# First batch's decays from sums of logarithms, its order written anew, and staged weights loaded next: one Trainium2 core

## The chip, the cores and the metric

The kernel runs on one core of a Trainium2 chip. The metric is the device time of one execution in microseconds (us), the median of several runs.

## What is computed

A gated linear attention feeds a mixer. Batch 4, 8 heads, 768 positions, head width 48; everything is float32, and the weights arrive as float64.

```
f = sigmoid(f_logit)
for t in range(S):
    state = f[t][:, None] * state + outer(k[t], v[t])     # for each batch and head, 48 x 48
    y[t]  = q[t] @ state
x = y as (batch, position, 384)
u = x + (x^T @ U @ V)^T                                   # rank 32, over the positions
out = u + relu(u @ w_ch1) @ w_ch2                         # 384 -> 1536 -> 384
```

## The kernel before

**Units.** A unit is two heads of one batch; a batch has HP = 4 units, all four have NU = 16. The 768 positions are cut into NCH = 12 chunks of 64, two chunks to a block of 128 (NBL = 6). Within a chunk the recurrence is written with two decays for each channel: X, the product of the gates from a position's successor to the end of the chunk, and Y, its counterpart for the queries, so that a key times X and a query times Y can be multiplied as matrices. `prepare(n)` (L643) makes them in five pieces: `gates` (L677) turns f with six transposes on TensorE and applies two sigmoids on ScalarE; `keep` (L692) makes X by a scan on VectorE that runs backwards (L694), copies the chunk totals to `least` (L699), and takes a floor, a reciprocal and a product for the later scan and the state (L701, L702, L704); `keys` (L706) turns k and multiplies it by X (L672); `read` (L710, under the name read_back in the order) makes Y by a second scan (L712); `queries` (L714) turns q and multiplies it by Y.

**Attention.** `attend(n)` (L770) has six pieces: `kept` (L802) turns the scaled keys back with twelve small transposes, copies them to kb (L813) and spreads the chunk totals to `whole` (L815); `states` (L817) multiplies kb by v and copies the sums to `added` (L833); `scan` (L838) carries the state over the chunks on VectorE (L848); `scores` (L780) multiplies keys by queries and masks them into A (L795); `read` (L855) multiplies the queries by the states (L865) and copies two columns to `seen` (L872); `inner` (L874) adds A times v (L883) and copies the result to x (L889). PSUM tiles of two banks rotate through three buffers (ps_big), and so a product waits until the tile of three before has been read.

**Order.** For the first batch the order is written out by hand (L979 to L998), and from there to the start of the second batch TensorE, VectorE and ScalarE execute exactly in the order of the program (manual_schedule, L966 and L967). `front(n, ...)` and `rear(n, ...)` fetch pieces of `prepare` and `attend`. `busy(3)` puts three filler products on TensorE in each turn. After the loop come the last unit's pieces, the weights of the low rank step and the mixer's start (L1001 to L1018); then the dense layer runs, `ch1` (L258) first, with the second batch's units between its pieces (L1024).

**Loads.** All loads are issued by SyncE, in program order: `load(n, names)` (L530) brings f, k, q, v of a unit. In the first batch each of f, k, q is loaded for the unit two later as soon as its own has been turned (`follow`, L651), v after the turn (L989).

**Weights.** Each weight slice is loaded raw as float64 and turned into float32 by `weight_loader`'s `end` (L83): two operations on ScalarE (L90, L91), three on VectorE (L92 to L94), one on GpSimd (L95). The list has U, two pieces of V (`early` = 3), twelve slices of w1 and twelve of w2. The first FIRST = 6 slices of w1 land in a tile of the dense layer that is still free (zw). Five weights are issued after the second turn (L993), four more after the loop (L997); from then on the end of one weight issues the one nine later (`ahead_by`, L103).

Of the kernel before, what the change touches and what calls it, by code (L numbers as in the profile page):

```python
# [10 lines left out]
F32 = mybir.dt.float32  # L11
# [14 lines left out]

LEAST = 1e-18

SMALLEST = struct.unpack("f", struct.pack("I", 896 << 20))[0]
# [443 lines left out]
def factored_path(ctx, tc, q, k, v, f_logit, moe_U, moe_V, moe_w_ch1, moe_w_ch2, out, ok):  # L473
# [49 lines left out]
    for slot in nat:  # L523
        for nm, t in slot.items():

            nc.gpsimd.memset(t[:, :, :, D:PAD], 20.0 if nm == "f" else 0.0)
    src = {"f": f_logit, "q": q, "k": k, "v": v}
# [30 lines left out]

    load(0, "f", "k", "q")
    load(1, "f")  # L560
    load(0, "v")
    load(1, "k", "q", "v")

    ident = const.tile([P, P], F32, name="ident")
# [33 lines left out]
    for i in range(2):  # L598
        nc.gpsimd.memset(wholes[i][:, 0:1], 0.0)

    table = one.tile([P, 1], F32, name="table")
    nc.scalar.activation(table, ident[:, 0:1], AF.Sigmoid)

# [39 lines left out]
    def prepare(n):  # L643
# [7 lines left out]
        def follow(nm):  # L651

            if n + 2 < NU and n + 2 not in (HP, HP + 1):
                load(n + 2, nm)
# [14 lines left out]
        def operand(nm, of):  # L669
            t = T[nm] = kz[n % 2][:, C:] if nm == "k" else two.tile([P, S], F32, name="qT")  # L670
            if n < TURNED:
                nc.vector.tensor_tensor(halves(t), on_tensor(nm), halves(T[of]), ALU.mult)  # L672
            else:
                turned(t, r[nm])
                nc.vector.tensor_tensor(t, t, T[of], ALU.mult)

        def gates():  # L677
# [36 lines left out]
        def queries():  # L714
            operand("q", "Y")
            follow("q")

        return [gates, keep, keys, read, queries]

# [247 lines left out]
    with tc.manual_schedule(engines={nc.vector.engine, nc.scalar.engine}):  # L967
# [4 lines left out]
        def busy(n):  # L972
            for _ in range(n):
                nc.tensor.matmul(idle[:, 0:DM], lhsT=ident, rhs=ends[:, 0:DM], start=True, stop=True)

        busy(1)
        for piece in front(0, "gates"):
            piece()
        for n in range(HP):  # L979
            pieces = front(n, "keep", "keys") + rear(n - 1, "scan", "scores")  # L980
            if n + 1 < HP:
                pieces += [lambda: busy(3)]
            pieces += rear(n, "kept") + front(n, "read_back", "queries")
            if n + 1 < HP:
                pieces += front(n + 1, "gates") + rear(n - 1, "read", "inner") + rear(n, "states")
            for piece in pieces:
                piece()
            if n < 2:
                load(n + 2, "v")  # L989
            if n == 1:  # L990


                for start, _ in weights[: early + 2]:  # L993
                    start()
            elif n > 1:
                load(n + 2, "f", "k", "q", "v")
        for start, _ in weights[early + 2 : early + FIRST]:  # L997
            start()  # L998


        loads = ahead_by(early + FIRST, weights)  # L1001
        done, rest = slice(0, 2 * n * D), slice(2 * n * D, DM)
        pieces = rear(n - 1, "read") + rear(n, "states") + rear(n - 1, "inner") + rear(n, "scan") + loads[:1]
        pieces += rear(n, "scores") + loads[1:2] + rear(n, "read") + loads[2 : early + 1]
        for piece in pieces:
# [3 lines left out]
        low_rank_of(done)  # L1009
        loads[early + 1]()  # L1010
        for piece in rear(HP - 1, "inner"):
# [3 lines left out]
        mix_of(done)  # L1015
        added_up_of(rest)
        mix_of(rest)
        loads = loads[early + 2 :]  # L1018

# [64 lines left out]
    lowest = one.tile([1, 1], F32, name="lowest")  # L1084
    nc.vector.tensor_reduce(lowest, lp[0:1, 0:P], AX.X, ALU.min)
    nc.vector.tensor_single_scalar(ok, lowest, LEAST, ALU.is_ge)
# [332 lines left out]
```

## Time and profile before

| | us |
|---|---|
| median of 3 runs | 485.11 |
| lowest, highest | 484.94, 485.13 |
| the profiled execution | 486.26 |
| its span, first to last instruction | 484.5 |
| PE busy in the span | 463.1 (96%) |
| VectorE busy | 358.2 (74%) |
| ScalarE busy | 170.7 (35%) |
| GpSimd busy | 37.7 (8%) |
| first dense matmul (L258) starts | 54.06 |

PE is TensorE's matmuls, PEld its weight loads, DVE is VectorE, ACT ScalarE, POOL GpSimd, SP SyncE. A busy PE is not PE at its peak, since matmuls are pipelined. A row of the groups names line, engine, operation, tiles and shapes; then busy time, mean ns of one, and the idle time before them with what ended it. A row of the timeline has start and length, and in brackets the idle time before it with its releaser.

### The profile page before, as it was taken

Reading aid. Unit: us, or ns where it says so; the run is one execution under the profiler, and the core shown is the slowest. Engines: PE = TensorE matmul, PEld = TensorE weight load, DVE = VectorE, ACT = ScalarE, POOL = GpSimd, SP = SyncE. Lnnn points to the kernel's source line nnn. Section 1 sums busy time; section 2 is a strip of 40 time slices with the busy share of each in tenths; the row PEclk is TensorE's granted clock in tenths of the full one; section 3 lists DMA queues with packets and bytes.
Section 4 is the critical chain, followed back from the end, with each engine's and each line's share of the span. In section 5 each row is a group of like instructions: output and inputs, shape, how many; then the busy total and the mean of one; then the engine's idle time right before and its main releaser. Section 6 shows DMA issues by size and latency. Waiting matters only on the chain.

```text
span 484.5 us, 12730 instructions
## 1 busy us (share of the span) xinstructions
PE 463.1 (96%) x5535; PEld 397.8 (82%) x5535; DVE 358.2 (74%) x563; ACT 170.7 (35%) x321; POOL 37.7 (8%) x49
## 2 busy tenths in 40 slices
PE   7897999999999899999999999999999999999995
PEld 4675788886666468799899888899979999999995
DVE  5988599778999847666766655997896886858642
ACT  2436475664444313433342304543221312112200
POOL 3001145444000000000000000000000000000000
PEclk9999899999999999999999999999999999999999
DMA  9977976757677613152526300100000000000001
GB/s 145 161 151 157 252 192 153 161 147 92 107 122 109 102 42 42 26 74 51 83 27 107 50 18 18 27 3 21 18 1 1 33 2 18 16 1 34 1 33 39
DMA packets 158679, 34.34 MB, mean 71 GB/s; under 512 B 149206, under 2 KB 157078, under 8 KB 158614
## 3 DMA queue, kind: packets, MB, share of 16 engines
q1 hardware_dynamic: 158614, 33.44, 37.4%
q8 instruction: 45, 0.74, 0.6%
q14 instruction: 20, 0.16, 0.1%
HBM read 28.70 MB, written 4.72 MB: 69 GB/s over the span
## 4 chain that ended last, share of the span: by engine, by line
PE 69%; DVE 16%; DMA 6%; ACT 3%; SPq 3%; issue 3%; POOL 0%; DVEq 0%; POOLq 0%; ACTq 0%
PE pw L312 26%; PE pz L258 17%; PE pp L410 11%; DVE late L712 2%; PE y L865 2%; DVE late L694 2%; PE y L883 2%; DMA late<-in_f_logit_dram 2%; PE pt L660 2%; PE po L283 2%; SPq L548 2%; PE sc L788 1%; DVE added L848 1%; DVE w_y L94 1%; PE put L246 1%
## 5 line engine op out<-in xcount | busy, mean ns | idle before, releaser
L258 PE MATMUL pz<-uT,w 128*128 128x256 f32 x504 | 115.5, 385 | 1.4 <-ACT z_all L268 1.1
L258 PEld LDWEIGHTS pz<-uT,w 128*128 128x128 f32 x504 | 94.6, 192 | 15.5 <-ACT z_all L268 1.5
L312 PE MATMUL pw<-w,z_all 128*128 128x192 f32 x216 | 37.7, 329 | 0.0
L312 PE MATMUL pw<-zw,w_raw 128*128 128x192 f32 x216 | 37.3, 327 | 0.0
L312 PEld LDWEIGHTS pw<-zw,w_raw 128*128 128x128 f32 x216 | 35.2, 190 | 0.8 <-DVE w_raw L187 0.6
L312 PEld LDWEIGHTS pw<-w,z_all 128*128 128x128 f32 x216 | 35.0, 190 | 0.7
L95 POOL TENSOR_TENSOR w<-w_y,w_r 128x384 int32<-128x384 int32 x24 | 31.5, 1313 | 41.5 <-DVE w_y L94 30.1
L694 DVE TENSOR_TENSOR_SCAN late<-fz,late 128x768 f32<-128x768 f32 x16 | 28.1, 1757 | 8.7 <-ACT fz L681 4.4
L268 ACT ACTIVATE z_all<-pz 128x512 f32<-128x512 f32 x33 | 19.7, 595 | 32.9 <-PE pz L258 32.8
L410 PE MATMUL pp<-v_nat,late 128*128 128x128 f32 x224 | 28.8, 275 | 0.0
L712 DVE TENSOR_TENSOR_SCAN late<-fz,other 128x768 f32<-128x768 f32 x16 | 28.0, 1747 | 0.2
L410 PEld LDWEIGHTS pp<-v_nat,late 128*128 128x128 f32 x224 | 27.0, 192 | 0.0
L283 PE MATMUL po<-w,z_all 128*128 128x384 f32 x72 | 24.9, 493 | 1.2 <-DVE o L187 1.2
L853 ACT COPY st<-added 128x576 f32<-128x576 f32 x12 | 14.7, 1224 | 30.5 <-DVE added L848 30.5
L403 ACT ACTIVATE other<-other 128x512 f32<-128x512 f32 x18 | 11.3, 631 | 39.9 <-DVE other L187 39.9
L283 PE MATMUL po<-w,zw 128*128 128x384 f32 x72 | 25.3, 496 | 0.0
L92 DVE TENSOR_SCALAR w_y<-w_y 128x384 f32<-128x384 f32 (+3 forms) x27 | 13.4, 496 | 13.6 <-ACT w_y L90 13.3
L795 DVE TENSOR_TENSOR A<-sc,causal 128x768 f32<-128x768 f32 x16 | 15.2, 947 | 10.5 <-PE sc L788 10.5
L283 PEld LDWEIGHTS po<-w,z_all 128*128 128x128 f32 x72 | 13.3, 190 | 10.1 <-DVE o L187 1.8
L283 PEld LDWEIGHTS po<-w,zw 128*128 128x128 f32 x72 | 13.1, 190 | 9.7 <-issue 1.2
L833 ACT COPY added<-ds 48x576 f32<-48x576 f32 (+1 forms) x28 | 17.8, 636 | 4.2 <-PE ds L826 3.8
L403 ACT ACTIVATE z_all<-z_all 128x512 f32<-128x512 f32 x12 | 7.6, 630 | 32.8 <-DVE z_all L187 32.8
(193 smaller groups left out, 833.4 us busy)
## 6 DMA issues: line engine op xcount, KB each, us to landing
w_raw<-in_moe_w_ch_dram SPq DMA_DIRECT2D x18, 384.0 KB, 4.0
out_dram<-o SPq DMA_DIRECT2D x24, 192.0 KB, 1.9
v_nat<-in_v_dram SPq DMA_DIRECT2D x16, 144.0 KB, 3.8
v_nat<-in_v_dram SPq DMA_DIRECT2D x32, 72.0 KB, 3.6
zw<-in_moe_w_ch_dram SPq DMA_DIRECT2D x6, 384.0 KB, 4.7
late<-in_f_logit_dram SPq DMA_DIRECT2D x10, 96.0 KB, 3.4
late<-in_k_dram SPq DMA_DIRECT2D x10, 96.0 KB, 3.2
late<-in_q_dram SPq DMA_DIRECT2D x10, 96.0 KB, 2.9
```

What stands on the lines that cost most here:

```text
L95: nc.gpsimd.tensor_tensor(dst.bitcast(I32), shaped(y.bitcast(I32)), shaped(r), ALU.add)
L258: nc.tensor.matmul(pm[:, i * 2 * P : (i + 1) * 2 * P], lhsT=w1[:, m, o : o + P], rhs=uT[a][:, m, :], start=(m == 0), stop=(m == NDC - 1))
L268: nc.scalar.activation(z[a, c][:, k : k + 2, :].rearrange("p i t -> p (i t)"), pm, AF.Relu)
L283: nc.tensor.matmul(pm, lhsT=z[a, i // NI][:, i % NI, s * P : (s + 1) * P], rhs=w2[:, i, :], start=(i == 0), stop=(i == NFC - 1))
L312: nc.tensor.matmul(pm[:, n * HM : (n + 1) * HM], lhsT=lhs[:, i, :], rhs=rhs[:, i, :], start=(i == 0), stop=(i == NI - 1))
L403: nc.scalar.activation(dst, dst, AF.Relu, scale=float(SIGNS[n]))
L410: nc.tensor.matmul(pm[:, i, r * P : (r + 1) * P], lhsT=room["w"](wn)[:, r * P : (r + 1) * P], rhs=x_node(a, xn), start=((xn, wn) == of[0]) ...
L694: nc.vector.tensor_tensor_scan(backwards(X, S - 1, S), backwards(f, S, S), backwards(ends, S - 1, S), 0.0, ALU.mult, ALU.add,)
L712: nc.vector.tensor_tensor_scan(Y, f[:, 0:S], starts, 0.0, ALU.mult, ALU.add)
L795: nc.vector.tensor_tensor(T["A"], sc[:, :, 0 : NBL * C].rearrange("p h (c i) -> p h c i", i=C), causal.unsqueeze(1).unsqueeze(1).broadcast ...
L833: nc.scalar.copy(added[r, 1:].rearrange("p (e c s) -> p e c s", c=NBL, s=2), ds[r, :, 0 : NBL * D].rearrange("p s (c e) -> p e c s", e=D),)
L853: nc.scalar.copy(st, states.rearrange(by_e, c=NCH))
```

## The change

For the units of the first batch the two decays come from logarithms. f is not turned first: it is clamped from below at FLOOR = -40, `exp(-f)` and `ln(1 + ...)` give the negative logarithm of the gate in place, and six products with a constant matrix `later` (128 x 130: ones where one position follows another in the same chunk, and two columns of whole chunks) give the sums after each position, already turned. `exp(-sum)` is X, `exp(sum)` is Y, and the two extra columns give the chunk totals. `prepare` returns [logs, keep_logs, keys, log_sums, queries] for n < HP and the old five otherwise. The filler products `busy(3)` are gone from the loop, the pieces of the loop stand in a new order, the loads of the units 2 and 3 are issued by the loop itself, and all nine staged weights are issued after the second turn, ahead of the loads of the units 4 and 5. The first two slices of w1 are turned into float32 after the second low rank product rather than before the first. The activation at the start that brings in a function table asks for Exp rather than Sigmoid and stands earlier.

```diff
-    load(0, "f", "k", "q")
+    load(0, "f", "k")
     load(1, "f")
-    load(0, "v")
+    load(0, "q", "v")
     load(1, "k", "q", "v")
+
+    table = one.tile([P, 1], F32, name="table")
+    nc.vector.memset(table, 0.0)
+    nc.scalar.activation(table, table, AF.Exp)
+
+    later = const.tile([P, P + 2], F32, name="later")
+    nc.vector.memset(later, 0.0)
+    for s in range(2):
+        half = later[s * C : (s + 1) * C, s * C : (s + 1) * C]
+        nc.vector.memset(half, 1.0)
+        nc.vector.memset(later[s * C : (s + 1) * C, P + s : P + s + 1], 1.0)
+        nc.gpsimd.affine_select(out=half, in_=half, compare_op=ALU.is_ge, fill=0.0, base=-1,
+                                pattern=[[-1, C]], channel_multiplier=1)
...
-    table = one.tile([P, 1], F32, name="table")
-    nc.scalar.activation(table, ident[:, 0:1], AF.Sigmoid)
...
-            if n + 2 < NU and n + 2 not in (HP, HP + 1):
+            if n >= HP and n + 2 < NU:
                 load(n + 2, nm)
...
+        def logs():
+            fn = nat[n % 2]["f"][:, :, :, 0:D]
+            nc.vector.tensor_single_scalar(fn, fn, FLOOR, ALU.max)
+            nc.scalar.activation(fn, fn, AF.Exp, scale=-1.0)
+            nc.scalar.activation(fn, fn, AF.Ln, bias=1.0)
+
+        def log_sums():
+            pt = T["sums"] = ps_big.tile([P, 2, 512], F32, name="pt", tag="big")
+            for c in range(NBL):
+                o = c % (NBL // 2) * (P + 2)
+                nc.tensor.matmul(
+                    pt[:, 2 * c // NBL, o : o + P + 2],
+                    lhsT=nat[n % 2]["f"][:, c].rearrange("p h d -> p (h d)"), rhs=later, start=True, stop=True,
+                )
+
+        def keep_logs():
+            by_block = T["sums"][:, :, 0 : NBL // 2 * (P + 2)].rearrange("p a (c t) -> p a c t", t=P + 2)
+
+            def blocks_of(t):
+                return t.rearrange("p (a c t) -> p a c t", a=2, t=P)
+
+            T["X"], T["Y"] = late[:, 4, :], late[:, 5, :]
+            nc.scalar.activation(blocks_of(T["X"]), by_block[:, :, :, 0:P], AF.Exp, scale=-1.0)
+            nc.scalar.activation(
+                least[:, n, :].rearrange("p (a c s) -> p a c s", a=2, s=2), by_block[:, :, :, P : P + 2], AF.Exp, scale=-1.0
+            )
+            nc.scalar.copy(wholes[n % 2][:, 1:NCH], least[:, n, 1:NCH])
+            nc.scalar.activation(blocks_of(T["Y"]), by_block[:, :, :, 0:P], AF.Exp)
...
+        if n < HP:
+            return [logs, keep_logs, keys, log_sums, queries]
         return [gates, keep, keys, read, queries]
...
-        for piece in front(0, "gates"):
+        for piece in front(0, "gates", "read_back", "keep"):
             piece()
+        load(2, "f")
         for n in range(HP):
-            pieces = front(n, "keep", "keys") + rear(n - 1, "scan", "scores")
+            early_on = n + 2 < HP
+            pieces = rear(n - 1, "scan") + front(n, "keys")
+            if early_on:
+                pieces += [lambda: load(n + 2, "k")]
+            pieces += rear(n - 1, "read") + rear(n, "kept")
             if n + 1 < HP:
-                pieces += [lambda: busy(3)]
-            pieces += rear(n, "kept") + front(n, "read_back", "queries")
+                pieces += front(n + 1, "gates")
+            pieces += rear(n - 1, "inner") + front(n, "queries")
             if n + 1 < HP:
-                pieces += front(n + 1, "gates") + rear(n - 1, "read", "inner") + rear(n, "states")
+                pieces += front(n + 1, "read_back", "keep")
+            if n + 3 < HP:
+                pieces += [lambda: load(n + 3, "f")]
+            if early_on:
+                pieces += [lambda: load(n + 2, "q", "v")]
+            pieces += rear(n, "scores", "states")
             for piece in pieces:
                 piece()
-            if n < 2:
-                load(n + 2, "v")
             if n == 1:
-                for start, _ in weights[: early + 2]:
+                for start, _ in weights[: early + FIRST]:
                     start()
             elif n > 1:
                 load(n + 2, "f", "k", "q", "v")
-        for start, _ in weights[early + 2 : early + FIRST]:
-            start()
...
-        pieces = rear(n - 1, "read") + rear(n, "states") + rear(n - 1, "inner") + rear(n, "scan") + loads[:1]
-        pieces += rear(n, "scores") + loads[1:2] + rear(n, "read") + loads[2 : early + 1]
+        pieces = rear(n, "scan") + loads[:1] + rear(n, "read") + loads[1:early]
...
         low_rank_of(done)
-        loads[early + 1]()
         for piece in rear(HP - 1, "inner"):
             piece()
         added_up_of(done)
         low_rank_of(rest)
         mix_of(done)
         added_up_of(rest)
+        loads[early]()
         mix_of(rest)
+        loads[early + 1]()
```

The other lines of the diff set the pad columns of f to 0 instead of 20 and leave the pad rows out of the smallest chunk total at the end.

More of the change, by code (lines that the diff above doesn't have):

```diff
@@ L27 @@
 LEAST = 1e-18
+FLOOR = -40.0
 SMALLEST = struct.unpack("f", struct.pack("I", 896 << 20))[0]
@@ L524, in factored_path @@
         for nm, t in slot.items():
-            nc.gpsimd.memset(t[:, :, :, D:PAD], 20.0 if nm == "f" else 0.0)
+            nc.gpsimd.memset(t[:, :, :, D:PAD], 0.0)
     src = {"f": f_logit, "q": q, "k": k, "v": v}
@@ L1084, in factored_path @@
     lowest = one.tile([1, 1], F32, name="lowest")
-    nc.vector.tensor_reduce(lowest, lp[0:1, 0:P], AX.X, ALU.min)
+    nc.vector.tensor_reduce(lowest, lp[0:1, 0:P].rearrange("o (h d) -> o h d", d=PAD)[:, :, 0:D], AX.XY, ALU.min)
     nc.vector.tensor_single_scalar(ok, lowest, LEAST, ALU.is_ge)
```

## The prediction, made before the changed kernel was run

> **What bounds the kernel now.** I read the granted clock first (0.995 over the span: nothing disturbed), then the stages, then the order of time around the change. The stages, with columns length, busy time of PE, PEld, DVE, ACT and POOL, granted clock, DMA share, GB/s:
>
> ```profile
> 10.00:20.00 10.00, 8.35 (x151) 6.12 (x150) 9.51 (x11) 4.47 (x8) 0.00 (x0) 1.00 1.33 160
> 20.00:30.00 10.00, 9.56 (x242) 7.63 (x246) 8.45 (x11) 3.91 (x9) 0.00 (x0) 1.00 0.80 142
> 30.00:40.00 10.00, 8.13 (x324) 7.07 (x317) 9.02 (x11) 4.46 (x10) 0.00 (x0) 1.00 0.79 180
> ...
> 50.00:60.00 10.00, 9.16 (x50) 7.54 (x51) 4.41 (x9) 4.14 (x9) 1.53 (x2) 0.83 1.15 263
> ```
>
> From about 54 us on TensorE runs the dense layer without a gap worth naming; the same work in the same order follows whatever happens before. So the change is worth what it moves the first dense matmul (54.06 us), plus what it saves in the stall just after it. Ahead of that, the first batch's four units are bound by VectorE (8.5 to 9.5 of each 10 us), while ScalarE has about half its time free. The scans are the largest groups there:
>
> ```profile
> L694 DVE TENSOR_TENSOR_SCAN late<-fz,late 128x768 f32<-128x768 f32 x16 | 28.1, 1757 | 8.7 <-ACT fz L681 4.4
> ...
> L712 DVE TENSOR_TENSOR_SCAN late<-fz,other 128x768 f32<-128x768 f32 x16 | 28.0, 1747 | 0.2
> ```
>
> One unit on ScalarE, in order of time (start, length), shows which of its steps the new ones must stand between:
>
> ```profile
> 28.48 0.80 ACT L813 COPY kb<-pt 128x768 f32<-128x768 f32 x1 [3.54 <-PE pt L809]
> 29.17 0.67 ACT L815 COPY whole<-whole 128x576 f32<-128x576 f32 x1
> 29.88 0.80 ACT L681 ACTIVATE fz<-pt 128x756 f32<-128x756 f32 x1
> 30.57 0.17 ACT L682 ACTIVATE f<-pt 128x12 f32<-128x12 f32 x1
> 31.05 0.16 ACT L872 COPY seen<-y 128x2 f32<-128x2 f32 x1 [0.30 <-PE y L865]
> 32.24 0.64 ACT L889 COPY x<-y 128x576 f32<-128x576 f32 x1 [1.03 <-PE y L883]
> 33.00 0.64 ACT L833 COPY added<-ds 128x576 f32<-128x576 f32 x1
> ```
>
> The stall after the start: the dense matmuls begin, and ScalarE stands 3.06 us before a weight that has not landed, with TensorE's next operand behind it in its queue; steady work starts at 61.74.
>
> ```profile
> 54.06 3.85 PE L258 MATMUL pz<-uT,w 128*128 128x256 f32 x12
> ...
> 56.87 0.55 ACT L90 ACTIVATE w_y<-zw 128x384 f32<-128x384 f32 x1 [3.06 <-DMA zw<-in_moe_w_ch_dram]
> ...
> 61.74 5.45 PE L258 MATMUL pz<-uT,w 128*128 128x256 f32 x24 [0.27 <-ACT uT L247]
> ```
>
> And the only table load of the program:
>
> ```profile
> 0.80 1.28 ACT L602 ACT_TABLE_LOAD   x1 [0.80 <-PEq L1403]
> ...
> 2.71 0.20 ACT L602 ACTIVATE table<-ident 128x1 f32<-128x1 f32 x1 [0.63 <-POOL ident masks.py:199]
> ```
>
> **What the Trainium skill says.** (1) "ScalarE: Activation LUTs", "What ACT_TABLE_LOAD costs" and "Table sets": a switch of function set is a load of about 1283 ns plus about 1380 ns of drain; the exponential's own set has no logarithm, and one set holds both. The trace agrees on the load (1.28 us) and shows no such drain: the first activation waits 0.63 us after it, for GpSimd. (2) "ScalarE activation tables", "Table sets in the compiler and the runtime": sets are chosen for the longest run of activations, which would pick the joint set. No trace here shows two functions of different sets. (3) "TensorE: Matmul & The Clock Gate", Part 1: half clock until a few us of activity. The trace agrees: six transposes take 1.51 us at 4.81 and 0.86 later, and the clock is 0.50 from 53 to 56 us. (4) "VectorE: DVE Perf Modes": an fp32 operation with a constant in SBUF runs two elements a cycle. It agrees: L92 takes 0.36 us for 384.
>
> **The change part by part, for each first-batch unit.**
>
> VectorE loses both scans (1.76 + 1.75), the floor, reciprocal and product of L701 to L704 (0.17 + 0.23 + 0.11), and gains a clamp of 576 elements (0.45 to 0.75 by the L92 row; I take 0.50). 8.2 us becomes 4.7.
>
> ScalarE loses the two sigmoids and the copy of X0 (0.80 + 0.17 + 0.21) and gains Exp and Ln over 576 elements (0.67 each, as L815), X and Y (0.80 each, as L681), and two operations on 12 elements (0.2 each). 4.1 becomes 6.3, without table loads.
>
> TensorE loses six transposes (0.86) and the three filler products (2.2); it gains six log-sum products, about 0.9.
>
> Setup and order of loads: two selects (0.23 each, as L578) and small fills go ahead of the identity on GpSimd and VectorE, which is needed first by k's transposes at about 9 us; without that cover 0.5. q of unit 0 now lands behind f of unit 1, at about 10 (four pairs at 1.8 each from 4.7), and is needed near 12. The loads of units 2 and 3 are issued in nearly the old order, and a slower loop is late for none of them: 0.
>
> Table loads: the new first activation asks for Exp alone; Ln follows, then Exp again, in every unit. Bounds: one load if the joint set is picked, eight in the first batch if each activation missing from the loaded set gets the first set that has it. One more for the Sigmoid of the second batch has ScalarE's spare time as cover; without that it costs 1.3 once. I take eight: the load that the trace has carries the line of the very activation it serves (L602), so it was placed at that instruction and not for a run of them. Each at 1.28; the other end is 2.66.
>
> Now the queue. In a turn of the new loop, ScalarE executes kb, whole, Exp, Ln of the next unit, x, X, the small two, Y, added. The state scan needs added; the read needs the scan; the kept transposes stand behind the read on TensorE; kb needs those. That is a **closed ring** in which ScalarE is never ahead: scan 1.35 + read 1.24 + kept 0.58 + kb 0.80 + whole 0.67 + Exp 0.67 + load 1.28 + Ln 0.67 + x 0.64 + load 1.28 + X 0.80 + small 0.40 + Y 0.80 + added 0.64 = 11.8, less about 0.1 at eight joints (whole starts 0.69 after kb, not 0.80): **11.0 us a turn**. Before, the scans of L694 start at 13.43, 21.90, 30.71: 8.5 and 8.8. The log sums (0.9) lie under the second load. DVE's gain buys nothing here.
>
> Unit 0: f lands at 4.8; clamp to 5.3, Exp 6.0, load 7.2, Ln 7.9, sums at half clock (1.5) 9.5, X, small, Y to 11.9; kept and kb, whole to 13.8; Exp, load, Ln of unit 1 to 16.2; load 17.4; X to Y 19.1; added 19.7. Then 30.7 and 41.7 (two turns). The last turn has no next unit: scan 1.35, read 1.24, kept 0.58, inner 0.92, q transposes 0.86, qT 0.96, scores 0.93, states 0.90, added 0.64 = 8.4: 50.1. Before, added ends at 14.0, 24.8, 33.6, 39.5.
>
> The tail: 39.5 to 54.06 is 14.5 before. After: scan 1.35, U's vector and GpSimd parts 1.4, low rank 1.5, inner 0.9, x 0.65, low rank of the rest 0.5, mix to the first add 0.8, adds 2.1, first w1 slice on DVE 1.3, adds 0.8, transposes 0.9, uT copy 0.8 = 13.0; the second slice of w1, moved behind, is later: DVE 1.3 and GpSimd 1.0 from 61.4 give 63.9, 0.8 more. Tail 13.8; first dense matmul at about **63.9: +9.9**.
>
> Weights: four w1 slices are issued before the inputs of units 4 and 5. All DMA is issued long before 63 us, so the 3.06 us wait goes. From 54.06 to 61.74 TensorE did 24 products and 6 transposes, 6.0 us at full clock; half of the rest is the cold clock, which stays. Gain 0.6 to 1.7, I take 1.2. The inputs behind the weights on SP's queue are needed some 13 us after the first dense matmul (66.8 before): cover enough; without it their 4 x 384 KB at 350 GB/s (the rate from 59 to 63 us) cost 4.5.
>
> Clock: with no filler, TensorE idles about 2 us twice a turn, and unit 0 is counted cold already. Bounds 0 to +6 (all of the ring's and tail's PE work a third longer); I take +1.5.
>
> Sum: +9.9 - 1.2 + 1.5 = **+10.2**. The profiled execution took 486.26 us (span 484.5, 1.8 around it), 1.15 above the median 485.11; it would become 496.5, the median **495.3**.
>
> **The rivals.**
>
> C, one joint set: the loads vanish, but then the sums (0.9, held by x, which frees their PSUM buffer) show. A turn is 11.0 less the two loads (2.4) plus the sums with their hand-overs (1.3): 9.9; unit 0 ends 2.4 earlier; together 2.4 + 2 x 1.1 = 4.6 less, 490.7 (488 to 493). Skill page (2) speaks for it. Chance 0.17.
>
> B, the clock stays low in half the windows: 498.5 to 503. For it: 0.50 at 53 us after a stretch recorded as 60 to 70% busy. Against: 40 to 50 us, just as busy, stayed at 1.00. 0.13.
>
> D, a drain of 1.38 at each of eight loads: +11, 506. 0.05; L602 speaks against it.
>
> E, **faster**: ScalarE isn't the ring I draw, as its copies overlap TensorE's work, and VectorE's 3.5 us come through until DMA is the limit. From f2's landing at 20.05 (18 of 32 blocks of 147 KB) and 165 GB/s, v of unit 3 lands at about 33.6; states, added and scan end at 36.5 instead of 40.92: -4.4, -0.7 in the tail, -1.2 in the stall: 478.8. It decides as soon as a turn is under 8.6 us. Even without any load ScalarE's steps in the ring sum to 6.1, its three others to 3.2 and the log sums to 0.9, so it is unlikely. 0.10, of which 0.02 ends within 0.2%.
>
> **How the numbers follow.** Forecast A (492.5 to 498.5) 0.55; B 0.13, C 0.17, D 0.05, E 0.10. 488.5 to 502 holds A, nearly all of C, three quarters of B: 0.8. Faster 0.08, within 0.2% (what a measurement of this kernel can tell) 0.02, slower 0.90.
>
> **What would show it.** Nine or so ACT_TABLE_LOAD rows by 70 us, two a unit; added ending near 20, 31, 42, 50; VectorE half idle from 10 to 50 us; the first L258 matmul near 64; no wait on DMA zw. Wrong if there are one or two loads (C), or if added is at 36 (E), or if transposes of six take 1.5 us in mid-phase (B).

## The result, and the profile after

The changed kernel takes **505.86 us** (median of 6 runs, 503.70 to 509.44) against 485.25 us for the kernel before in the same comparison: a ratio of 1.0396, 95% interval [1.0328, 1.0464]. It is slower, as forecast, but by about 20 us where 10 were forecast, and above the range. The profiled execution took 503.70 us, the lowest of the six; its span is 501.9 us (before 484.5), its mean granted clock 0.984 (before 0.995). In the changed kernel the dense product stands at L259, the clamp, Exp and Ln at L690 to L692, the log sums at L698, X and Y at L710 and L715, the copies of kb, the totals and the sums `added` at L855, L857 and L875.

The stages again: length, busy time of PE, PEld, DVE, ACT and POOL, granted clock, DMA share, GB/s.

```profile
10.00:20.00 10.00, 6.31 (x37) 5.39 (x36) 2.28 (x3) 6.67 (x11) 0.00 (x0) 1.00 1.30 152
20.00:30.00 10.00, 8.48 (x190) 7.78 (x193) 3.53 (x4) 3.79 (x8) 0.00 (x0) 0.91 0.54 99
30.00:40.00 10.00, 6.91 (x196) 6.12 (x192) 4.17 (x5) 7.63 (x12) 0.00 (x0) 0.92 0.73 156
40.00:50.00 10.00, 7.61 (x197) 6.83 (x189) 2.12 (x3) 7.83 (x13) 0.00 (x0) 0.83 1.01 265
...
60.00:70.00 10.00, 8.72 (x145) 5.72 (x145) 5.03 (x14) 3.62 (x12) 1.49 (x3) 0.71 0.78 207
```

From 10 to 50 us VectorE went from 8.3 to 9.5 of each 10 us down to 2.1 to 4.2: what the change aimed at was achieved. Nothing took its place as a full engine: ScalarE is busy for 3.8 to 7.8 of 10. No engine is the bound any more; a ring of waits is. Transfers aren't the bound either: after the first f, no engine waits for an input ahead of the dense layer.

The clock column has to be read with care. It says 1.00 over the first 28 us, yet there six log-sum products took 2.97 us, twice, and 1.61 at 33.58, where it says 1.00 too. "Half clock" below is said of products that took nearly twice the time of their like, whether or not the column shows it.

In place of the two groups of scans stand these groups of the first 75 us (shapes kept apart):

```profile
L698 PE MATMUL pt<-later,other 128*128 128x130 f32 x24 | 5.7, 427 | 5.0 <-ACT other L692 5.0
L692 ACT ACT_TABLE_LOAD x4 | 5.1, 1283 | 0.1
L710 ACT ACT_TABLE_LOAD x4 | 5.1, 1283 | 0.1
...
L710 ACT ACTIVATE late<-pt 128x768 f32<-128x768 f32 x4 | 3.2, 811 | 4.5 <-PE pt L698 4.5
```

Eight loads of 1.28 us in the first batch, as forecast. But the last row says that X stood 4.5 us in all before the log sums; in the forecast it did so only in unit 0, for about 0.3. One whole turn on ScalarE (start, length, idle time before it and its releaser) shows the ring:

```profile
40.53 0.16 ACT L914 COPY seen<-y 128x2 f32<-128x2 f32 x1 [2.81 <-PE y L907]
41.05 0.80 ACT L855 COPY kb<-pt 128x768 f32<-128x768 f32 x1 [0.36 <-PE pt L851]
41.74 0.67 ACT L857 COPY whole<-whole 128x576 f32<-128x576 f32 x1
42.32 0.69 ACT L691 ACTIVATE other<-other 128x576 f32<-128x576 f32 x1
43.02 1.28 ACT L692 ACT_TABLE_LOAD   x1
44.31 0.68 ACT L692 ACTIVATE other<-other 128x576 f32<-128x576 f32 x1
44.90 0.62 ACT L931 COPY x<-y 128x576 f32<-128x576 f32 x1
45.54 1.28 ACT L710 ACT_TABLE_LOAD   x1
47.84 0.81 ACT L710 ACTIVATE late<-pt 128x768 f32<-128x768 f32 x1 [1.02 <-PE pt L698]
48.55 0.18 ACT L711 ACTIVATE least<-pt 128x12 f32<-128x12 f32 x1
48.75 0.20 ACT L714 COPY whole<-least 128x11 f32<-128x11 f32 x1
48.86 0.81 ACT L715 ACTIVATE late<-pt 128x768 f32<-128x768 f32 x1
49.85 0.64 ACT L875 COPY added<-ds 128x576 f32<-128x576 f32 x1 [0.19 <-PE ds L868]
```

From kb to `added` ScalarE pauses only for the sums (1.02) and briefly for the states (0.19), and then waits 2.81 us for scan and read, which themselves wait for `added`: it is idle because it is the link that holds up its own supply.

The four copies `added` end at 25.82, 37.71, 50.49 and 58.95; before, they ended at 14.04, 24.83, 33.64 and 39.53. So the lag is 11.8 us after the first unit, then 12.9, 16.9 and 19.4: more than half of it arises in the first unit. And the start of the dense layer:

```profile
73.28 2.94 PE L259 MATMUL pz<-uT,w 128*128 128x256 f32 x12 [0.33 <-ACT uT L248]
76.72 7.93 PE L259 MATMUL pz<-uT,w 128*128 128x256 f32 x36
```

The first dense product starts 19.2 us later (73.28 for 54.06), but the wait for a landing weight is gone: the first 48 products end 11.4 us after the first one's start (84.65), before 13.1 after it (67.19). 19.2 less 1.8 is 17.4, the whole difference of the two spans. The time is lost ahead of the dense layer and nowhere else.

### The profile page after: what moved, and what is told of

Its sections match the earlier page's. It is cut to its first block, busy times and chain, and to the rows that moved or that the text cites. A ratio compares the mean times of both kernels' runs of the same rounds, so it can differ in the third digit from the quotient of the medians.

```text
span 501.9 us, 12771 instructions
## 1 busy us (share of the span) xinstructions
PE 466.5 (93%) x5541; PEld 404.1 (81%) x5541; DVE 346.3 (69%) x553; ACT 190.2 (38%) x342; POOL 38.1 (8%) x51
## 4 chain that ended last, share of the span: by engine, by line
PE 70%; DVE 15%; ACT 6%; DMA 3%; issue 3%; SPq 2%; DVEq 0%; ACTq 0%
PE pw L313 25%; PE pz L259 18%; PE pp L411 11%; PE y L907 2%; DVE late L752 2%; PE sc L830 2%; PE y L925 2%; PE pt L698 2%; DVE late L734 2%; PE po L284 2%; PE put L247 1%; PE pt L851 1%; DVE added L890 1%; DMA other<-in_f_logit_dram 1%; PE ds L868 1%
## 5 line engine op out<-in xcount | busy, mean ns | idle before, releaser
L259 PE MATMUL pz<-uT,w 128*128 128x256 f32 x504 | 114.3, 382 | 1.4 <-ACT z_all L269 1.1
L259 PEld LDWEIGHTS pz<-uT,w 128*128 128x128 f32 x504 | 93.8, 190 | 14.9 <-ACT z_all L269 1.5
L269 ACT ACTIVATE z_all<-pz 128x512 f32<-128x512 f32 x33 | 19.7, 597 | 34.1 <-PE pz L259 34.1
L404 ACT ACTIVATE other<-other 128x512 f32<-128x512 f32 x18 | 11.3, 631 | 39.9 <-DVE other L188 39.9
L734 DVE TENSOR_TENSOR_SCAN late<-fz,late 128x768 f32<-128x768 f32 x12 | 21.1, 1755 | 4.0 <-ACT fz L729 3.6
L907 PEld LDWEIGHTS y<-st,qT 48*64 48x64 f32 x704 | 14.0, 142 | 11.6 <-issue 10.0
L907 PE MATMUL y<-st,qT 48*64 48x48 f32 x704 | 16.1, 234 | 6.4 <-DVE st L890 4.1
L284 PEld LDWEIGHTS po<-w,z_all 128*128 128x128 f32 x72 | 13.3, 190 | 10.1 <-DVE o L188 1.8
L752 DVE TENSOR_TENSOR_SCAN late<-fz,other 128x768 f32<-128x768 f32 x12 | 21.0, 1746 | 0.2
L284 PEld LDWEIGHTS po<-w,zw 128*128 128x128 f32 x72 | 13.1, 190 | 9.7 <-issue 1.2
```

The lines of the kernel that those rows point to most:

```text
L259: nc.tensor.matmul(pm[:, i * 2 * P : (i + 1) * 2 * P], lhsT=w1[:, m, o : o + P], rhs=uT[a][:, m, :], start=(m == 0), stop=(m == NDC - 1))
L269: nc.scalar.activation(z[a, c][:, k : k + 2, :].rearrange("p i t -> p (i t)"), pm, AF.Relu)
L284: nc.tensor.matmul(pm, lhsT=z[a, i // NI][:, i % NI, s * P : (s + 1) * P], rhs=w2[:, i, :], start=(i == 0), stop=(i == NFC - 1))
L734: nc.vector.tensor_tensor_scan(backwards(X, S - 1, S), backwards(f, S, S), backwards(ends, S - 1, S), 0.0, ALU.mult, ALU.add,)
L752: nc.vector.tensor_tensor_scan(Y, f[:, 0:S], starts, 0.0, ALU.mult, ALU.add)
L907: nc.tensor.matmul(o(c % 2, par, c // 2), lhsT=T["q"][rows[par], chunk[c]], rhs=T["st"][rows[par], c, :], start=(c <= 2), stop=False, skip ...
```

## The experiments

The theory at this point: the ring is what the forecast drew, eight loads in it without a drain, and its terms were too small, since the log sums take 1.6 to 3.0 us rather than 0.9, and the first clamp 1.81 rather than 0.5. Rivals: a load costs more on the path than its 1.28 us; the low clock is the main cause; the ring isn't ScalarE's.

**One set for both functions.** One line ahead of the first activation; nothing else changes.

```diff
+    nc.scalar.preload_act_table_set("natural_log_exp_and_others")
     nc.scalar.activation(table, table, AF.Exp)
```

> Edit: the joint exponential-and-logarithm set is loaded at the start, so the eight switches of the first batch go (two loads remain: this one and the sigmoid's). Theory ring (ScalarE is in a closed ring with all its loads): the load ahead of Ln goes from every unit's path (4 x 1.28), the one ahead of X only as far as it is longer than the log sums it lies beside (3.0 cold, 1.6 warm, so little): 5 to 7 less, 499 to 501; a turn falls from 12.3 to about 10.8. Rival clock (a half clock of TensorE is what costs): the loads lie beside slow products, under 3 less, above 503. Rival drain: each load costs 2.66 with its drain, over 12 less, below 494.

Measured: 497.45 us, ratio 1.0244 [1.0209, 1.0278], 8.4 us under the changed kernel (7.4 by the ratios), more than the 5 to 7 of the theory. The loads that remain are the first and the one for the second batch's sigmoid:

```profile
0.80 1.28 ACT L567 ACT_TABLE_LOAD   x1 [0.80 <-PEq L1450]
80.21 1.28 ACT L722 ACT_TABLE_LOAD   x1
```

Eight loads are thus worth about 1 us each, less than their 1.28, since other waits come out where they stood: X of the first two units now waits 3.06 us for its sums instead of 1.76. Not all of the gain is the loads': the sums of the fourth unit also fell from 2.75 us to 1.61. The rival with a drain beside each load asked for over 12.

**Fillers back in the loop.** The three filler products ahead of the log sums in each turn but the last.

```diff
             if n + 1 < HP:
+                pieces += [lambda: busy(3)]
                 pieces += front(n + 1, "read_back", "keep")
```

> Edit: the three filler products are put back into each of the first three turns, ahead of the log sums. Rival clock: the granted clock stays at 1.00 from 25 to 70 us, the sums of units 2 and 3 take 1.6 instead of up to 2.75, the tail's products are half as long: 6 or more less, below 500. Theory ring: only the products in the ring get shorter (sums of one turn by 1.1, read and kept of another by 1, the tail by 1 to 1.5): 2 to 4 less, 502 to 504. If the fillers delay the sums instead: 1 to 3 more.

Measured: 502.85 us, 1.0344 [1.0316, 1.0373], 3.0 less in the medians, as the ring theory had it; the interval overlaps the changed kernel's. In its trace the sums of the second and fourth unit fell from 2.97 and 2.75 us to 1.61. From 50 to 60 us, where there is still no filler, its clock was 0.53.

**States ahead of the next unit's sums.** The pieces `scores` and `states` of this unit come before the next unit's `log_sums` and `keep_logs`, so that ScalarE copies `added` before X and Y.

```diff
+            pieces += rear(n, "scores", "states")
             if n + 1 < HP:
                 pieces += front(n + 1, "read_back", "keep")
...
-            pieces += rear(n, "scores", "states")
```

> Edit: scores and states of a unit stand ahead of the next unit's log sums and X, Y; loads and sizes as in the changed kernel. Theory ring: added no longer waits for the sums, X and Y of the next unit (sums 1.6 to 3.0, X to Y 1.8), so scan, read and kept lie beside them, and a turn is what ScalarE executes plus the wait for the sums, about 9.5 instead of 12.3: 6 to 9 less, 497 to 500. Rival clock: the order changes nothing that the clock sets, under 2 less; the granted clock is low in the same stretches.

Measured: 493.93 us, 1.0167 [1.0150, 1.0184]: 11.9 less, more than expected, with every load and every sum still there. A stage of its trace:

```profile
30.00:40.00 10.00, 7.57 (x232) 6.54 (x236) 4.60 (x5) 9.16 (x17) 0.00 (x0) 1.00 0.86 239
```

Its ScalarE copies `added` first and turns to X afterwards:

```profile
27.04 0.62 ACT L931 COPY x<-y 128x576 f32<-128x576 f32 x1
27.69 0.64 ACT L875 COPY added<-ds 128x576 f32<-128x576 f32 x1
28.35 1.28 ACT L710 ACT_TABLE_LOAD   x1
29.65 0.81 ACT L710 ACTIVATE late<-pt 128x768 f32<-128x768 f32 x1
```

ScalarE is now busy 9.16 of 10 us (7.63 in the changed kernel), a turn takes 9.0 us (`added` starts at 18.68, 27.69, 36.72), and the clock is 1.00 up to 40 us. The second load, the wait for the sums, X and Y did little harm as mere work; they were dear because they stood between the read of one unit and its next state. (The load ahead of Ln still stands there.) This is the largest effect of a single edit.

Part of it comes through the clock. The first unit's products were at full clock from about 12.5 us, in the changed kernel from about 24.5, although the two programs are the same up to there (k's transposes, at 12 us in both, took 1.08 and 1.49). When the clock rises thus varies from run to run. The order's effect doesn't hang on that alone: all four runs lie between 493.04 and 494.08, the lowest of the changed kernel is 503.70.

**Weights alone.** The kernel before, with its nine staged weights issued together after the second turn as in the change.

```diff
-                for start, _ in weights[: early + 2]:
+                for start, _ in weights[: early + FIRST]:
                     start()
...
-        for start, _ in weights[early + 2 : early + FIRST]:
-            start()
```

> Edit: the kernel before, with all nine staged weights issued after the second turn and nothing else changed. From the trace of the changed kernel (48 dense products and 6 transposes in 11.2 us, 13.1 before): 1 to 2 less than the kernel before, 483 to 484. Rival: the weights push the inputs of units 4 and 5 and the tail's U and V have to share the DMA with them, so no gain or up to 2 more.

Measured: 487.48 us (14 runs), 1.0028 [1.0014, 1.0042]: 1.6 us more in the medians where 1 to 2 less were expected; the rival, no gain or up to 2 more, held. The stall is gone in its trace (48 dense products from 55.63 to 66.88, 11.3 us), but they start 1.6 later. A row of the kernel before, and the same one here:

```profile
40.43 0.61 PE L883 MATMUL y<-v_nat,A 64*64 64x48 f32 x27 [1.31 <-issue]
```

```profile
42.11 0.61 PE L883 MATMUL y<-v_nat,A 64*64 64x48 f32 x27 [2.47 <-issue]
```

TensorE has a gap inside these products in which it waits for nothing that the profile shows; it grew by 1.16 us while the weights were moving (202 GB/s from 40 to 50 us, 141 before). That their transfers caused it is argued, not shown. This profiled execution (485.88) was the fastest of the 14, so what the median lost beyond it isn't seen.

**The sums twice.** Each log-sum product is made a second time.

```diff
-            for c in range(NBL):
+            for c in list(range(NBL)) * 2:
```

> Edit: each unit's log sums are computed twice in a row into the same place (the second overwrites the first with the same numbers). Theory (the sums lie on the path once they outlast the load beside them): X of unit 0 and 1 moves by 3.0 each at half clock, of units 2 and 3 by 1.6 to 2.7: 6 to 9 more than the changed kernel, 512 to 515. Rival (they lie under the load ahead of X, as the prediction had it): under 3 more, below 509. If the added work keeps the clock up, a gain of 1 to 2 is taken off either.

Measured: 512.46 us, 1.0543 [1.0526, 1.0559]: 6.6 more. Two of its doubled groups:

```profile
9.22 4.81 PE L698 MATMUL pt<-later,late 128*128 128x130 f32 x24 [3.70 <-ACT late L692]
20.55 5.57 PE L698 MATMUL pt<-later,other 128*128 128x130 f32 x24 [3.23 <-ACT other L692]
```

The groups of all four units sum to 19.7 us (10.3 in the changed kernel). Most of the 9.4 us that were added came through: what makes the sums longer isn't hidden under a load.

**GpSimd's fills moved.** The fills of `starts` and fz go to VectorE, after the first clamp.

```diff
-    nc.gpsimd.memset(starts, 0.0)
...
-    for i in range(2):
-        nc.gpsimd.memset(fz[i], 0.0)
...
+        for t in (starts, fz[0], fz[1]):
+            nc.vector.memset(t, 0.0)
         load(2, "f")
```

> Edit: the fills of starts and of the two fz tiles move from GpSimd, where they run from 3.8 to 5.9 us, to VectorE after the first unit's clamp. Theory (the first clamp takes 1.81 instead of 0.45 because GpSimd's fills run at the same time): the clamp takes 0.45 to 0.5, everything after it 1.3 earlier, 504 to 505. Rival (the first clamp is long because its input is still landing or because it is the first of its kind): it stays at 1.8, no change.

Measured: 503.17 us, 1.0370 [1.0341, 1.0399], 2.7 less in the medians, which the intervals don't separate. The trace is clearer. The first clamp of the changed kernel, with GpSimd's fills in the same stretch, and here:

```profile
4.64 1.81 DVE L690 TENSOR_SCALAR late<-late 128x576 f32<-128x576 f32 x1 [2.10 <-DMA late<-in_f_logit_dram]
```

```profile
3.76 0.74 POOL L598 MEMSET other<- 128x768 f32 x1
4.44 1.42 POOL L602 MEMSET fz<- 128x769 f32 x2
```

```profile
4.68 0.46 DVE L687 TENSOR_SCALAR late<-late 128x576 f32<-128x576 f32 x1 [2.14 <-DMA late<-in_f_logit_dram]
```

The clamp takes 0.46 us when the fills are gone, and the first sums start 1.3 earlier (7.91 for 9.21). Only 0.3 of that reaches the dense layer in this trace (72.95 for 73.28): the granted clock is 0.67 and 0.70 from 20 to 40 us, 0.91 and 0.92 in the changed kernel. The Trainium skill's "SBUF — State Buffer", "SBUF: two separate sides", says that VectorE in its two-port mode and GpSimd exclude each other from a shared pair of ports for a whole instruction. The numbers fit it within 0.13 us: the fills end at 5.86, plus 0.46 is 6.32, and the clamp ended at 6.45. The kernel before showed the same effect already, in the conversion of weights, on VectorE alone and beside GpSimd:

```profile
46.48 0.36 DVE L93 TENSOR_SCALAR w_y<-w_y 128x384 uint32<-128x384 uint32 x1
...
47.58 1.00 POOL L95 TENSOR_TENSOR w<-w_y,w_r 128x384 int32<-128x384 int32 x1 [1.35 <-ACT w_r L91]
47.73 1.05 DVE L93 TENSOR_SCALAR w_y<-w_y 128x384 uint32<-128x384 uint32 x1
```

**Set and order together.** The edits of the first and third experiment.

> Edit: the joint set loaded at the start and scores and states ahead of the next unit's sums, both of the edits measured singly. In the run with the order alone ScalarE works through a turn of 9.0 without a gap, 2.6 of it loads. Theory (the ring is broken and ScalarE's sum is the bound): a turn falls to 6.8 to 7.4, unit 0 ends 1.3 earlier: 7 to 8 less than with the order alone, 486 to 487. Rival (the gains overlap, DMA or the sums take over): a turn stays at 8 or more, 489 to 491.

Measured: 492.24 us, 1.0134 [1.0113, 1.0155]. The theory failed and the rival held in the turns, 8.6 to 9.1 us (`added` starts at 19.69, 28.76, 37.34, 46.03); the time lies just above its 489 to 491. Once `added` comes ahead of X and Y, taking out the loads gained only 1.7 us, and the two intervals touch. That is not all the loads' doing: X of the first unit starts 1.3 us earlier than with the order alone (10.96 for 12.23), yet `added` 1.0 later (19.69 for 18.68), since this time the first unit's products ran at half clock until about 20 us.

Set against the first experiment, the same run shows the order without any loads in the way: 492.24 for 497.45, 5.2 less. There a turn at full clock took 10.1 us (`added` starts at 22.01 and 32.15), here 8.6. What remains is a ring through TensorE (kept, inner, q's transposes, a wait of 1.21 for VectorE's queries, scores, states, sums, k's transposes, read), no shorter than the 8.5 to 8.8 that VectorE's scans set before.

**All of it.** Set, order, fills moved, two fillers at the start (one before), three between the last states and the tail.

```diff
-        busy(1)
+        busy(2)
         for piece in front(0, "gates", "read_back", "keep"):
...
+        busy(3)
         pieces = rear(n, "scan") + loads[:1] + rear(n, "read") + loads[1:early]
```

> Edit: as the run before, and the fills moved, one more filler product at the start, and three between the last unit's states and the tail. Theory: clamp 1.3 earlier, the first sums at full clock for part of their time (0.5 to 1.5), the tail's products and the first dense ones at full clock (1.5 to 3): 3 to 5 less than the run before, 481 to 484, ahead of the kernel before. Rival (the input's landing bounds a unit's turn, so what is won early is waited away): 485 to 487, not ahead of it.

Measured: 486.00 us (22 runs), 1.0005 [0.9991, 1.0018]: level with the kernel before, not ahead; the theory failed. The rival's number held, but not its reason: TensorE waits 1.21 us in a turn for VectorE's queries, and the one late input, for which VectorE waits 0.8 us, doesn't hold up ScalarE's Exp behind it. In the first unit the sums now follow the fillers without a pause (at 6.78) and what comes after them runs at full clock: its `added` starts at 15.21 instead of 19.69. Of these 4.5 us 1.3 are the clamp's; k's transposes (0.82 for 1.49), q's (0.88 for 1.54), scores (0.93 for 1.56) and states (0.87 for 1.48) show where most of the rest comes from. In the profiled run (487.72, 1.7 above the median) the clock fell again just ahead of the dense layer, whose first twelve products took

```profile
55.56 4.74 PE L259 MATMUL pz<-uT,w 128*128 128x256 f32 x12
```

**Logarithms further ahead.** The last kernel with Exp and Ln of the next unit ahead of kb on ScalarE, the sums again ahead of scores and states, and f of unit 2 loaded ahead of q and v of unit 1.

```diff
-    load(1, "k", "q", "v")
+    load(1, "k")
...
         load(2, "f")
+        load(1, "q", "v")
...
-            pieces += rear(n - 1, "read") + rear(n, "kept")
+            pieces += rear(n - 1, "read")
             if n + 1 < HP:
                 pieces += front(n + 1, "gates")
+            pieces += rear(n, "kept")
             pieces += rear(n - 1, "inner") + front(n, "queries")
-            pieces += rear(n, "scores", "states")
             if n + 1 < HP:
                 pieces += front(n + 1, "read_back", "keep")
+            pieces += rear(n, "scores", "states")
```

> The e8_all kernel with ScalarE's order changed once more: Exp and Ln of the next unit ahead of this unit's kb and whole, the sums ahead of scores and states, and f of unit 2 loaded ahead of q and v of unit 1. Theory (what is left in the ring is order, no longer loads): the next unit's logarithms leave the ring, a turn takes 7.4 to 8.0 us where it took 8.6 to 9.1, and the kernel comes 2 to 4 us below e8_all, at 482 to 484 us. Rival (the ring is now TensorE's chain of kept, inner, scores, states and read, whatever ScalarE does first): the turn stays at 8.6 and the time at 485 to 487.

Measured: 494.17 us (490.47 to 497.78), 1.0138 [1.0081, 1.0196]: more than the kernel it builds on (6.5 by ratio, 8.2 by median) instead of 2 to 4 less. Neither theory nor rival foresaw that. Its ScalarE:

```profile
26.39 0.81 ACT L708 ACTIVATE late<-pt 128x768 f32<-128x768 f32 x1 [3.00 <-PE pt L696]
...
27.41 0.81 ACT L713 ACTIVATE late<-pt 128x768 f32<-128x768 f32 x1
28.11 0.63 ACT L873 COPY added<-ds 128x576 f32<-128x576 f32 x1
31.56 0.16 ACT L912 COPY seen<-y 128x2 f32<-128x2 f32 x1 [2.81 <-PE y L905]
```

`added` stands behind the sums, X and Y again, and the turns are 11.5, 10.4 and 11.6 us (the state scans start at 17.23, 28.78, 39.19 and 50.80) with no table load in them. Much of that is the clock: it was 0.69 from 20 to 30 us (2.72 us for the sums of unit 2) and 0.50 from 40 to 50, where the last turn of 11.6 has no next unit's sums in it at all; the turn of 10.4 contains a pause of 1.29 us within the states in which TensorE waited for nothing that the profile shows. So this run doesn't separate the order from the clock, nor the share of the two transfers that the edit moved; the order alone is seen in the two runs with the joint set, above.

**Two fillers in the tail**, after the second addition of the low rank part and after the last mix: first with the kernel just told, then with the one before it.

```diff
         added_up_of(rest)
+        busy(1)
         loads[early]()
         mix_of(rest)
+        busy(1)
         loads[early + 1]()
```

> The e9_logs_ahead kernel with a filler product after the last added state and one after the last mix, so that TensorE does not idle in the tail. Theory (the half clock at the start of the dense stage comes of the tail's idle TensorE): clock 1.00 into the dense products, the first twelve at 2.6 us where e8_all had 4.74, 1.5 to 2.5 us less than e9_logs_ahead. Rival (the clock there does not answer to two fillers, and they only stand ahead of the tail's products): the same as e9_logs_ahead or up to 1.4 us more.

Measured: 491.86 us, 1.0143 [1.0083, 1.0202], which its spread (490.58 to 497.91) doesn't tell from the same kernel without them. Inconclusive in time (turns of 10.1 us in its profile); the first twelve products took 2.96 us, 4.08 without.

> The e8_all kernel with the two fillers of the tail alone, its order otherwise kept. Theory (clock at the start of the dense stage): 1.5 to 2.5 us less than e8_all, 483.5 to 485 us. Rival (fillers only delay): no change, or up to 1.4 us more.

Measured: 485.35 us (21 runs), 0.9973 [0.9959, 0.9988]. The median is only 0.65 lower than without the two fillers; against the kernel before of its own comparison (486.32), the ratio falls from 1.0005 to 0.9973, 1.6 us, at the low end of the 1.5 to 2.5 expected. Its dense layer:

```profile
53.57 3.16 PE L259 MATMUL pz<-uT,w 128*128 128x256 f32 x12 [0.33 <-ACT uT L248]
57.22 7.94 PE L259 MATMUL pz<-uT,w 128*128 128x256 f32 x36
```

This is the only version faster than the kernel before, by 0.3%. The profiled run, 484.46, is the fastest of the 21. Its states are no earlier (the last `added` ends at 40.77, before 39.5); the dense layer starts 0.5 earlier, and 48 products end at 65.16 instead of 67.19, the stall being gone. So in this trace what it gains is the staged weights' and the tail's; the first batch's states, which the scans were taken out to hasten, come 1.2 us later.

**Clock alone.** The changed kernel with its own order and loads, the loop's fillers, two at the start and three ahead of the tail.

> The changed kernel with fillers alone: those of the loop back in all turns, two at the start and three ahead of the tail; its loads, sums and order stay. Theory (loads and order are the larger part, the clock some 3 to 6 us of the 20): 499 to 502 us. Rival (the clock is the main cause, and order and loads matter only because TensorE idles in them): under 495 us.

Measured: 502.36 us, 1.0329 [1.0276, 1.0382], 3.5 less than the changed kernel, just outside the 499 to 502 of the theory and far from the rival's 495. The profiled run was the fastest of five (499.53):

```profile
10.00:60.00 50.00, 42.46 (x879) 34.43 (x879) 18.47 (x22) 29.82 (x52) 0.59 (x1) 0.93 0.97 174
60.00:70.00 10.00, 7.66 (x112) 5.16 (x107) 7.82 (x18) 6.17 (x17) 2.46 (x4) 1.00 0.63 176
```

The tail's clock is 1.00 (0.71 in the changed kernel), and the kernel is still 3.3% slower than before. The turns show that the clock isn't the main cause: with the sums at 1.50 to 1.61 us they are still 12.0 and 12.2 (`added` starts at 22.90, 34.93, 47.13). But 3.5 is not the clock's whole share. The first unit ran at half clock here as well (sums 2.97, k's transposes 1.49, kept 0.90), and the fillers themselves held up the fourth unit's sums by 1.0 us (Ln ends at 42.84, the sums start at 43.87). What half clock puts on the first unit's path, 1.4 for the sums, 0.6 and 0.3 for the other two, makes about 2 us more, an estimate from these durations and their like at full clock (1.61, 0.88, 0.59).

Taken one on another, as ratios to the kernel before (a step's size depends on what was mended ahead of it: the set alone is worth 1.5%, but 0.3% once the order is mended, and every step shifts the clock too):

| kernel | ratio | step, us of 485 |
|---|---|---|
| the change | 1.0396 | |
| states ahead of the sums | 1.0167 | -11.1 |
| and one set | 1.0134 | -1.6 |
| and fills moved, fillers at the start and ahead of the tail | 1.0005 | -6.3 |
| and two fillers in the tail | 0.9973 | -1.6 |

## Why the prediction went wrong

**Right.** Slower, and by this mechanism: eight loads of 1.28 us and no drain (in unit 0 Exp ends at 7.17, a load starts at 7.18, and Ln at 8.48, just as it ends); an eager choice of sets rather than the joint one, against rival C, although the Trainium skill's "ScalarE: Activation LUTs", "Table sets: the hidden batching unit", counts one load for Ln and Exp; a closed ring in which ScalarE's copies stand between read and next state; VectorE half idle and nothing gained by it; the load for the sigmoid hidden (86.20 us); no wait on zw; the last turn of 8.5 us (8.4 forecast) and the tail of 14.3 (13.8). Rival E, faster, had no hold: no turn of any changed version was clearly under 8.5 us, with or without loads. Rival D named 506, next to the 505.86 measured, but its reason, a drain at each load, isn't there: that number is luck. Of rival B's sign, slow transposes in mid-phase, a part showed (q's took 1.54 us at 15.42 and 1.21 at 30.93).

**Wrong: the size of the ring's terms, above all of the log sums, and their place under the load.** The first dense product was forecast at 63.9, with 1.5 for the clock 65.4, and came at 73.28. The 7.9 us are found like this:

*"It gains six log-sum products, about 0.9"* and *"The log sums (0.9) lie under the second load"*. The price is that of six transposes (0.86). But each fp32 product of `later` leaves two records: 12 for six products, 1.61 us at full clock, 2.97 at half. Three of the four groups of the changed kernel:

```profile
9.21 2.97 PE L698 MATMUL pt<-later,late 128*128 128x130 f32 x12 [3.69 <-ACT late L692]
19.53 2.97 PE L698 MATMUL pt<-later,other 128*128 128x130 f32 x12 [2.57 <-ACT other L692]
...
33.58 1.61 PE L698 MATMUL pt<-later,late 128*128 128x130 f32 x12 [1.44 <-ACT late L692]
```

Only the last of these fits under x and load (0.62 and 1.28). X waited for the others 1.76, 1.76 and, in the fourth unit, 1.02 us. The experiment with doubled sums showed that what lengthens them is on the path.

*"I take 0.50"* for the clamp: right for three of them (0.45), 1.3 too little for the first, which GpSimd's fills held up. What the forecast said of fills (*"small fills go ahead of the identity"*, *"without that cover 0.5"*) was about new ones and their place in the queues. The three large fills that GpSimd had before as well stand in no term, nor what two engines share, although the kernel before showed it (0.36 and 1.05 us, above).

*"Unit 0 ... added 19.7"* became 25.82: Y ended 2.1 later than forecast (1.3 for the clamp and 1.5 for the sums, less 0.6 because X to Y took 1.8 us and not the 2.4 that the forecast had here, against 1.7 in unit 1), the next Exp another 0.9 (k's transposes 1.49 and kept 0.90, both at half clock), its Ln 0.3, Y of unit 1 another 2.0 (sums at half clock again), `added` 0.8 (states at half clock, 1.35). That is 6.1. *"11.0 us a turn"*, the ring itself, became 11.9 and 12.8: 0.9 for kept at half clock and hand-overs in the first; in the second 1.2 for sums and states, the rest hand-overs. That is 2.7 more. The last turn and the tail add 0.6, and 1.5 had been allowed for the clock.

*"Clock ... I take +1.5"*: the half clock sits inside most of the terms above. With fillers put back it is about 3 to 3.5 us in the medians (with intervals that touch the changed kernel's), within the bounds of 0 to 6 but twice what was taken; and in both of these experiments the first unit's sums still took 2.96 and 2.97 us. The forecast treated the missing fillers and the sums as two small terms. They can feed each other, a slow sum making the turn longer and the longer turn idling TensorE; that is argued, no run separates it.

*"Gain 0.6 to 1.7, I take 1.2"* for the weights: 1.8 in this trace. But in the kernel before the same edit cost 1.6 in the medians: "all DMA is issued long before" put no price on issuing it while TensorE works.

Two small slips of the forecast's sums change nothing: 63.9 is 9.8 above 54.06, not 9.9, and rival E's last input would land at 32.6, not 33.6 (14 blocks of 147 KB at 165 GB/s from 20.05).

The net in the profiled run, 7.9 less 0.6, is, but for rounding, the 7.2 us between the forecast 496.5 and 503.7; the median lies another 2.2 above that run, and before's profiled run had lain 1.2 above its median.

**Open.** What lengthens the gap within L883 while weights move; how much of the slow order with the logarithms ahead is its order, its clock and its moved transfers; how much of the order's 11 us comes through the clock; why runs of the changed kernel spread over 5.7 us (a varying clock is likely but not shown: the longest, 509.44, has the lowest mean clock, 0.954, but one of 503.73 has 0.975 and one of 505.99 has 0.986).

## What to carry to other kernels

Before work is moved from the busy engine to one with half its time free, draw the chain from a state to the next state and see which steps of the free engine stand in it: there each microsecond counts in full, and the engine's idle time is only the wait for its own result. Put what closes the chain (here `added`) ahead of what serves the next unit; that alone gave back 11 of the 20 us, part of it through the clock, and 5 where no load stood in the way. Price a new matrix product from a product of its type and its clock, not from a transpose of its size, and where fillers are taken out, price the whole chain at half clock as the other bound.

## What the hardware showed that was not expected

- A VectorE clamp of 128 x 576 took 1.81 us while GpSimd's fills ran and 0.46 without them.
- Six fp32 products of 128 x 130 left 12 records and took 1.61 us, six transposes of 128 x 128 left 6 and took 0.86; at half clock 2.97 and 1.49.
- The granted clock fell to about half in stretches of two to five us ahead of which TensorE had paused (0.50 at 46 to 48 and at 60 to 65 us in the changed kernel, after pauses of 2.39 and 2.29), though not after every pause (1.00 from 50 to 58 us, after one of 1.44 us). Two fillers in the tail went with 3.16 instead of 4.74 us for the first twelve dense products (one profile each, the one without them of a slower run than the median, the other of the fastest).
- At the start the same instructions ran at full clock from about 12.5 us in one trace and from about 24.5 in another, the clock column reading 1.00 in both.
- ACT_TABLE_LOAD took 1.28 us with no pause on either side (7.17, 7.18 to 8.46, 8.48), and Exp, Ln, Exp brought one at every switch until the joint set was asked for.
- A gap in TensorE's issue was 1.31 us in one trace and 2.47 where more weights were in flight; the cause isn't shown.
